# Order of VectorE's work in the ticks that hold both a mix and a last-stage piece

## The chip, the cores and the metric

The kernel runs on one core of a Trainium2 chip. The metric is the device time of one execution in microseconds (us), as the median of several runs. Views of the trace count time from the first instruction of the span. The engines are TensorE (PE for its matmuls, PEld for its weight loads), VectorE (DVE), ScalarE (ACT), GpSimd (POOL) and SyncE (SP, which only issues DMAs).

## The reference, cut to what matters

```python
X = np.fft.rfft(x, axis=1)                 # x: 4 x 3008 x 256, along the sequence
Yr = Xr @ w_r - Xi @ w_i + b_r             # the "mix"
Yi = Xr @ w_i + Xi @ w_r + b_i
Yr = np.sign(Yr) * np.maximum(np.abs(Yr) - 0.01, 0.0)   # soft threshold, Yi likewise
y = np.fft.irfft(Yr + 1j * Yi, n=3008, axis=1)
h = y.reshape(12032, 256) @ w_in           # 256 -> 2048
out = (h / (1 + np.exp(-h))) @ w_out       # 2048 -> 256
```

The soft threshold is computed as y minus y clipped to plus and minus 0.01.

## The kernel before, in words

The Fourier transform and its inverse are each done in two stages of small matmuls, with scratch in DRAM between the stages. Behind them comes the MLP, over 24 blocks of 512 of the 12032 rows (the last has 256), each in 16 slices of the hidden dimension. A block and a slice make one **tick**, and the main loop at the end of the kernel runs over some 380 ticks. Up to block 10 a tick sends to TensorE, in this order: the first product of this tick (`mlp1`, six matmuls of L599), what the schedule `fill` holds for the tick, and the second product of the tick two before (`mlp2`, eight matmuls of L757 and L761). A tick so filled is 4.5 to 6.5 us of TensorE's time.

All engines take their instructions in the order in which the program issues them; `manual_schedule` leaves that order alone. What `fill` holds is set by a planner ahead of the loop, one thing a tick:

- `stack_product` (a "piece" of the forward transform): two matmuls (L293) into two PSUM banks, each followed by a ScalarE copy (L294) and a VectorE addition (L295). Before it stands `stack_split`, a ScalarE copy (L283) and a VectorE subtraction (L284).
- `u3_step` half 0, a "step": `s2_3` (eight matmuls, L390, into one bank, read by ScalarE at L398 and L399 and by VectorE at L400 and L402), `split_z` (L447, L448), and `i1` (six matmuls, L462, into the next bank, copied by ScalarE at L466). The first three steps of a batch have no `i1`, the last three have no `s2_3`.
- `u3_step` half 1, a "mix" (`mix3`): 18 matmuls (L415). The first six go to one bank, which ScalarE copies to the tile q (L421); POOL adds the biases there (L422, L423). The other twelve go to a second bank, `pv`. What is left is the closure `shrink`, which is put on the list `deferred`: four VectorE additions of q and `pv` (L434, 64x256 each), a clip (L437) and a subtraction (L438). After the four additions the second bank is free.

`bank()` gives the banks of these three in turn from two tags, d0 and d1, of one bank each. So a piece or a step that stands in the tick after a mix takes for its first bank the one that q was copied from, and for its second bank the mix's `pv`.

The last stage of the inverse transform builds the next block's input for the MLP, in three calls a block: `i2` for each half of the 256 columns, and `i2_ends` for the remainder of the block before and the block's last, partial piece of the transform. `i2` is four to eight matmuls (L524, L531) into a bank of the tag h, a ScalarE copy (L559) and a VectorE subtraction (L563). `i2_ends` first does L559 and L563 on the remainder in SBUF (`rest`), then the matmuls, L559 and L563 on the new bank (`i2e`), and last a ScalarE copy of what is over into a new `rest` (L579). `mlp1` takes its banks from the same tag h, which has two.

The planner puts some of these calls into a tick that has a mix or a step already. They then have the time t + 0.5 in `fill`, and stand behind the second product on TensorE. There are 20 such ticks, in blocks 2, 3 and 5 to 9 (they prepare blocks 3, 4 and 6 to 10). In 19 of them the other occupant is a mix; in one it is a step. Of the 19, 13 hold an `i2` and six an `i2_ends`. Of the tick that follows,

- eight hold a `stack_product` (six of them after an `i2`, two after an `i2_ends`),
- eight hold a step with both `s2_3` and `i1` (six after an `i2`, two after an `i2_ends`),
- three hold a step with only one of the two, which takes only the first bank (one after an `i2`, two after an `i2_ends`).

In the loop before, the closures on `deferred` are called at the top of the next tick, ahead of `split_g` (ScalarE's L615 and VectorE's L616 of the tick before):

```python
while deferred:
    deferred.pop(0)()
if t and ticks[t - 1][0] not in FAST:
    split_g(*ticks[t - 1])
```

Of the kernel before, what the change touches and what calls it, by code (L numbers as in the profile page):

```python
# [149 lines left out]
def spectral_mlp_kernel(ctx: ExitStack, tc: tile.TileContext, x, w_r, w_i, b_r, b_i, w_in, w_out, c1, c2, c3, c4, c3f, c5, out):  # L150
# [43 lines left out]
    def flush(n):  # L194
        for dst, src in stores[:n]:
            nc.sync.dma_start(out=dst, in_=src)
        del stores[:n]
# [208 lines left out]
    deferred = []  # L406
# [185 lines left out]
    def mlp1(i, f):  # L592
        n = BLOCKS[i][1]
        h, l = xt[i]
        p = ps.tile([128, 512], F32, tag="h", bufs=2, name="h")
        m = 0
        for e in range(2):
            for w, v in ((win[0], h), (win[1], h), (win[0], l)):
                nc.tensor.matmul(  # L599
                    out=p[:, :n], lhsT=w[:, e, f * 128:(f + 1) * 128], rhs=v[:, e, :n],  # L600
                    start=(m == 0), stop=(m == 5),
                )
                m += 1
        g = sb.tile([128, 512], F32, tag="g", bufs=3, name="g")
        for q in halves(i, f):
            nc.scalar.activation(out=g[:, q], in_=p[:, q], func=ACTF.Silu)  # L606
        gf[i, f] = g

    def split_g(i, f):
        n = BLOCKS[i][1]  # L610
        g = gf[i, f]
        gh = sb.tile([128, 512], F32R, tag="gh", bufs=3, name="gh")
        gl = sb.tile([128, 512], F32R, tag="gl", bufs=3, name="gl")
        for q in halves(i, f):
            nc.scalar.copy(gh[:, q], g[:, q])  # L615
            nc.vector.tensor_sub(gl[:, q], g[:, q], gh[:, q])  # L616
        gf[i, f] = (gh, gl)
        units.extend((i, f, t) for t in range(n // 128))
# [71 lines left out]
    def fast_one(i, q):  # L690

        px = fast_bank()
        fast_product(px[:, 0:HB], i, q, 0, 0, True)
        fast_product(px[:, HB:BLK], i, q, 1, 1, False)
        fast.append([i, q, px])

    def fast_more():

        i, q, px = fast[-1]
        py = fast_bank()  # L700
        fast_product(py[:, 0:HB], i, q, (0, 0), (0, 0), True)
        fast_product(py[:, HB:BLK], i, q, 2, 2, False)
        u = tl.tile([128, HB], F32, tag="u", bufs=2, name="u")
        g = tl.tile([128, 4, HB], F32, tag="gp", bufs=3, name="gp")
        nc.scalar.copy(u, py[:, 0:HB])
        nc.vector.tensor_tensor(out=u, in0=px[:, HB:BLK], in1=u, op=ALU.add)
        nc.vector.tensor_tensor(out=g[:, 3, :], in0=px[:, 0:HB], in1=u, op=ALU.add)
        nc.vector.tensor_tensor(out=g[:, 3, :], in0=py[:, HB:BLK], in1=g[:, 3, :], op=ALU.add)
        fast[-1] += [u, py, g]

    def fast_two():

        i, q, px, u, py, g = fast.pop(0)
        fast_product(px[:, 0:HB], i, q, 3, (1, 1), False)
        nc.vector.tensor_tensor(out=g[:, 1, :], in0=px[:, 0:HB], in1=u, op=ALU.add)  # L715
        fast_product(py[:, 0:HB], i, q, (1, 0), (1, 0), False)
        fast_product(py[:, HB:BLK], i, q, (1, 1), 3, False)
        nc.scalar.activation(out=g[:, 1, :], in_=g[:, 1, :], func=ACTF.Silu)  # L718
        nc.scalar.activation(out=g[:, 0, :], in_=py[:, 0:HB], func=ACTF.Silu)  # L719
        nc.vector.tensor_tensor(out=g[:, 2, :], in0=py[:, HB:BLK], in1=u, op=ALU.add)  # L720

        def parts(r):
            h, l = [tl.tile([128, 2, HB], F32R, tag=f"g{k}", bufs=4, name=f"g{k}") for k in "hl"]
            v = g[:, 2 * r:2 * r + 2, :]
            if r:
                nc.scalar.activation(out=v, in_=v, func=ACTF.Silu)  # L726
            nc.scalar.copy(h, v)  # L727
            nc.vector.tensor_sub(l, v, h)  # L728
            gf[i, 2 * q + r] = tuple(a.rearrange("p a c -> p (a c)") for a in (h, l))
            units.extend((i, 2 * q + r, t) for t in range(BLK // 128))  # L730

        parts(0)
        later.append(lambda: parts(1))
# [114 lines left out]
    with tc.manual_schedule():  # L848
# [154 lines left out]
        fill = {}  # L1003
# [14 lines left out]
        def last_stage(i, first):  # L1018

            at(first - 2, i2_load, i)  # L1020
            put(first, i2, i, 0)
            put(first + 2, i2, i, 1)
            at(first + 2, i2_load, i, True)
            return put(first + 4, i2_ends, i)
# [29 lines left out]
        done, t, since = 37, 24, 0  # L1054
# [38 lines left out]
        for i in range(FAST[0], len(BLOCKS)):  # L1093
            if i in FAST:
                first = max(16 * i - 13, last + 1)
                t = last_stage(i, first)
# [19 lines left out]
        def fills(t):  # L1116
            for fn, args in fill.pop(t, []):
                fn(*args)
            if t == int(t):
                flush(1 if t < 12 else 4)  # L1120

        def run(n):
            for v in units[:n]:
                mlp2(*v)
            del units[:n]

        def rest_of_pair():
            while later:
                later.pop(0)()

        first_fast, last_fast = 16 * FAST[0], 16 * (FAST[-1] + 1)
        for t in range(len(ticks) + 1):
            i, f = ticks[t] if t < len(ticks) else (LAST, None)
# [4 lines that stand above are left out]
            if i in FAST:  # L1138
                q = t - first_fast
                if f % 2 == 0:  # L1140
                    state["fast"] = True
                    fast_one(i, f // 2)
                    run(2)
                    if q:
                        fast_two()
                        run(2 if q > 2 else 0)
                else:
                    fast_more()
                    if f != 3:
                        rest_of_pair()  # L1150
                    run(2 if q < 4 else 4)
                    rest_of_pair()
                fills(t)
                continue
            if t == last_fast:
                run(2)
                fast_two()
                run(3)
                rest_of_pair()
            if f is not None:  # L1160
                mlp1(i, f)
            fills(t)
            if last_fast <= t < last_fast + 3:
                run(3 if t == last_fast else 4)
            else:
                run(sum(v[:2] != ticks[t - 1] for v in units))
            fills(t + 0.5)
        run(len(units))
        for k, (dst, src) in enumerate(stores):
            eng = nc.scalar if k % 2 else nc.sync  # L1170
# [28 lines left out]
```

## Time and profile before

| | |
|---|---|
| median of 3 runs | 1353.79 us |
| lowest and highest | 1353.29, 1356.28 us |
| the profiled execution | 1358.12 us |
| its span, first to last instruction | 1355.0 us |
| mean granted clock of TensorE | 0.997 |
| TensorE matmuls busy | 1327.7 us, 98% of the span |
| VectorE busy | 892.1 us, 66% |
| ScalarE busy | 803.7 us, 59% |

The profiled execution holds the span and 3.1 us around it. A row of a timeline has the start, the duration, the engine, the line, the operation, the tiles (out<-in), the shape and the count; in brackets stand the engine's idle time before the row and what ended it.

### The profile page before, as it was taken

The page shows a single profiled execution, that of the slowest core. Times are in us where ns is not written, and L with a number is a line of the kernel's source. Part 1 is how long each engine was busy: PE and PEld are TensorE (multiplying, and loading weights), DVE is VectorE, ACT ScalarE, POOL GpSimd, SP SyncE. Part 2 cuts the span into 40 slices and gives each one's busy share as a digit, 9 for nine tenths or more (in the row PEclk, how much of TensorE's full clock was granted, in tenths as well). Part 3 has the DMA queues.
Part 4 walks back from the last instruction along what each step waited for, and adds up shares of the span by engine and source line. Part 5 has one row for each costly group of instructions (what it writes and reads, how often), then busy time and mean ns, then how long its engine had stood idle before and what let it go on. Part 6 is the DMA issues. An engine that isn't in the chain of part 4 may idle for free.

```text
span 1355.0 us, 22638 instructions
## 1 busy us (share of the span) xinstructions
PE 1327.7 (98%) x8365; PEld 1180.3 (87%) x8365; DVE 892.1 (66%) x1704; ACT 803.7 (59%) x1690; POOL 209.7 (15%) x312
## 2 busy tenths in 40 slices
PE   8989999999999999999999999999999999999998
PEld 3967888888888888888988889999999999999998
DVE  3867746776666777756656756666666666666663
ACT  5546555655676766654554656666666665666555
POOL 2001002221112222111210102111111111111100
PEclk9999999999999999999999999999999999999999
DMA  8875514352436554332331110011001100110000
GB/s 267 264 217 176 140 54 110 97 138 65 114 101 170 126 129 124 93 115 81 106 93 38 46 31 4 28 31 31 7 17 46 31 19 14 31 31 13 5 23 24
DMA packets 76123, 109.98 MB, mean 81 GB/s; under 512 B 8854, under 2 KB 54798, under 8 KB 76014
## 3 DMA queue, kind: packets, MB, share of 16 engines
q1 hardware_dynamic: 61895, 79.17, 20.3%
q0 software_dynamic: 10544, 25.68, 7.8%
q10 hardware_dynamic: 3575, 3.70, 0.9%
q8 instruction: 66, 1.08, 0.3%
q14 instruction: 43, 0.35, 0.1%
HBM read 71.03 MB, written 37.49 MB: 80 GB/s over the span
## 4 chain that ended last, share of the span: by engine, by line
PE 92%; DMA 4%; DVE 2%; ACT 1%; issue 1%; SPq 0%; ACTq 0%; DVEq 0%
PE acc L757 25%; PE h L599 18%; PE h L680 17%; PE acc L761 13%; PE mix L415 6%; PE s L390 2%; PE i L462 2%; PE i2e L531 2%; PE i L531 1%; PE mix L354 1%; DMA scr<-i1o 1%; PE s L293 1%; DVE y L434 1%; DMA scr<-s1o 1%; PE acc L752 1%; DMA t3f<-in_c3f_dram 1%
## 5 line engine op out<-in xcount | busy, mean ns | idle before, releaser
L757 PE MATMUL acc<-wout,gh 128*128 128x512 f32 x1472 | 539.7, 397 | 0.3 <-ACT gh L615 0.3
L761 PE MATMUL acc<-wout,gl 128*128 128x256 f32 x1472 | 414.0, 281 | 0.2 <-DVE gl L616 0.2
L757 PEld LDWEIGHTS acc<-wout,gh 128*128 128x128 f32 x1472 | 278.2, 189 | 48.5 <-ACT gh L615 0.5
L599 PE MATMUL h<-xt,win 128*128 128x512 f32 (+1 forms) x1152 | 290.8, 388 | 0.0
L761 PEld LDWEIGHTS acc<-wout,gl 128*128 128x128 f32 x1472 | 277.5, 189 | 4.6 <-DVE gl L616 0.5
L599 PEld LDWEIGHTS h<-xt,win 128*128 128x128 f32 x1152 | 198.6, 188 | 39.5 <-DVE xt L563 0.4
L606 ACT ACTIVATE g<-h 128x512 f32<-128x512 f32 (+2 forms) x193 | 111.4, 578 | 170.5 <-PE h L599 168.9
L616 DVE TENSOR_TENSOR gl<-g,gh 128x512 fp32r<-128x512 f32 (+2 forms) x193 | 128.2, 666 | 57.0 <-ACT gh L615 55.4
L728 DVE TENSOR_TENSOR gl<-gp,gh 128x512 fp32r<-128x512 f32 x192 | 137.1, 714 | 29.4 <-ACT gh L727 29.4
L718 ACT ACTIVATE gp<-gp 128x256 f32<-128x256 f32 x96 | 40.1, 417 | 163.4 <-DVE gp L715 163.4
L727 ACT CAST gh<-gp 128x512 fp32r<-128x512 f32 x192 | 119.0, 620 | 6.1
L615 ACT CAST gh<-g 128x512 fp32r<-128x512 f32 (+2 forms) x193 | 116.2, 602 | 1.4
L680 PE MATMUL h<-xt,win 128*128 128x256 f32 x576 | 100.7, 284 | 0.5 <-DVE gp L715 0.5
L422 POOL TENSOR_TENSOR q<-q,bias 128x256 f32<-128x256 f32 x36 | 30.9, 859 | 383.1 <-ACT q L421 373.8
L720 DVE TENSOR_TENSOR gp<-h,u 128x256 f32<-128x256 f32 x96 | 40.8, 425 | 72.6 <-ACT gp L719 72.6
L680 PEld LDWEIGHTS h<-xt,win 128*128 128x128 f32 x576 | 81.9, 189 | 5.0 <-DVE gp L715 1.0
L680 PE MATMUL h<-th,sw_h 128*128 128x256 f32 x288 | 84.3, 293 | 0.0
L680 PE MATMUL h<-th,sw_l 128*128 128x256 f32 x288 | 81.6, 283 | 0.0
L680 PE MATMUL h<-tl,sw_h 128*128 128x256 f32 x288 | 81.0, 281 | 0.0
L434 DVE TENSOR_TENSOR y<-q,mix 64x256 f32<-64x256 f32 x144 | 60.3, 419 | 22.1 <-PE mix L415 16.8
L715 DVE TENSOR_TENSOR gp<-h,u 128x256 f32<-128x256 f32 x96 | 40.7, 424 | 50.4 <-PE h L680 50.1
L726 ACT ACTIVATE gp<-gp 128x512 f32<-128x512 f32 x96 | 61.3, 638 | 0.0
(175 smaller groups left out, 2375.3 us busy)
## 6 DMA issues: line engine op xcount, KB each, us to landing
a<-scr SPq DMA_DIRECT2D x48, 256.0 KB
x_sb<-in_x_dram POOLq DMA_DIRECT2D x64, 188.0 KB, 3.8
gin<-scr SPq DMA_DIRECT2D x48, 192.0 KB
t<-in_c_dram POOLq DMA_DIRECT2D x36, 256.0 KB, 3.6
scr<-i1o SPq DMA_DIRECT2D x36, 256.0 KB
t<-in_c_dram SPq DMA_DIRECT2D x48, 128.0 KB
scr<-s1o SPq DMA_DIRECT2D x32, 192.0 KB
scr<-s1o SPq DMA_DIRECT2D x13, 384.0 KB
```

Of the source, the lines that this page charges most:

```text
L415: nc.tensor.matmul(out=out, lhsT=x_[:, e, c, :], rhs=m[:, e, :], start=(n == 0), stop=(n == 5))
L434: nc.vector.tensor_tensor(out=y[64 * i:64 * i + 64, r, :], in0=q[rows, i, :], in1=pv[rows, i, :], op=op,)
L599: nc.tensor.matmul(out=p[:, :n], lhsT=w[:, e, f * 128:(f + 1) * 128], rhs=v[:, e, :n], start=(m == 0), stop=(m == 5),)
L606: nc.scalar.activation(out=g[:, q], in_=p[:, q], func=ACTF.Silu)
L615: nc.scalar.copy(gh[:, q], g[:, q])
L616: nc.vector.tensor_sub(gl[:, q], g[:, q], gh[:, q])
L680: nc.tensor.matmul(out=p, lhsT=w[j], rhs=m[k], start=(begins and n == 0), stop=(n == 2), skip_group_check=True,)
L726: nc.scalar.activation(out=v, in_=v, func=ACTF.Silu)
L727: nc.scalar.copy(h, v)
L728: nc.vector.tensor_sub(l, v, h)
L757: nc.tensor.matmul(out=a, lhsT=gh[:, q], rhs=wout[:, f].rearrange("p a c -> p (a c)"), start=begins, stop=False,)
L761: nc.tensor.matmul(out=a[:, D:2 * D], lhsT=gl[:, q], rhs=wout[:, f, 0, :], start=False, stop=ends,)
```

## The change

In a tick that has something at t + 0.5, the closures on `deferred` are called ahead of it, and no longer at the top of the next tick. So in the 19 shared ticks with a mix, the six VectorE instructions of `shrink` stand ahead of the L563 of the piece (in `i2_ends`, ahead of both). In all other ticks the program is the same. No instruction is added or taken away, and the order on every other engine and on every DMA queue stays.

```diff
                 run(sum(v[:2] != ticks[t - 1] for v in units))
-            fills(t + 0.5)
+            if t + 0.5 in fill:
+                while deferred:
+                    deferred.pop(0)()
+                fills(t + 0.5)
         run(len(units))
```

## Rows read from the trace of the kernel before

**Rows 1.** The page, busy time, share of the span and instructions of each engine.

```profile
PE 1327.7 (98%) x8365; PEld 1180.3 (87%) x8365; DVE 892.1 (66%) x1704; ACT 803.7 (59%) x1690; POOL 209.7 (15%) x312
```

**Rows 2.** The waits of PE: who waited for whom, us in total, times, longest.

```profile
PE s L293 <- DVE y L434: 8.8, 8, 1.3
PE i L462 <- PE s L390: 4.5, 8, 0.8
```

**Rows 3.** Groups by form, DVE, 200 to 735 us: busy us, mean ns | idle before.

```profile
L434 DVE TENSOR_TENSOR y<-q,mix 64x256 f32<-64x256 f32 x144 | 60.3, 419 | 22.1 <-PE mix L415 16.8 <-POOL q L422 3.4
...
L438 DVE TENSOR_TENSOR y<-y,q 128x512 f32<-128x512 f32 x36 | 24.9, 693 | 1.2
...
L437 DVE TENSOR_SCALAR q<-y 128x512 f32<-128x512 f32 x36 | 15.4, 428 | 1.2
```

**Rows 4.** Timeline of a mix that shares its tick with nothing, 200 to 215.

```profile
201.60 0.74 POOL L423 TENSOR_TENSOR q<-q,bias 128x256 f32<-128x256 f32 x1
...
201.84 1.72 DVE L434 TENSOR_TENSOR y<-q,mix 64x256 f32<-64x256 f32 x4 [2.43 <-PE mix L415]
```

**Rows 5.** Timelines of POOL, DVE and PE: a shared tick (i2), then stack_product.

```profile
298.53 1.21 POOL L422 TENSOR_TENSOR q<-q,bias 128x256 f32<-128x256 f32 x1 [11.79 <-ACT q L421]
299.81 0.73 POOL L423 TENSOR_TENSOR q<-q,bias 128x256 f32<-128x256 f32 x1
...
301.39 0.40 DVE L563 TENSOR_TENSOR xt<-i,xt 128x235 fp32r<-128x235 f32 x1 [2.25 <-ACT xt L559]
...
302.19 0.40 PE L293 MATMUL s<-sx,c_sb 111*128 111x512 f32 x1
303.67 0.47 PE L293 MATMUL s<-sx,c_sb 111*128 111x512 f32 x1 [1.08 <-DVE y L434]
303.98 0.40 PE L757 MATMUL acc<-wout,gh 128*128 128x512 f32 x1
```

**Rows 6.** Timeline of PE: a stack_product and a step without a wait.

```profile
519.27 0.63 PE L293 MATMUL s<-sx,c_sb 111*128 111x512 f32 x2
519.74 0.39 PE L757 MATMUL acc<-wout,gh 128*128 128x512 f32 x1
...
251.65 1.05 PE L390 MATMUL s<-t,a 128*128 128x128 f32 x8
252.46 0.36 PE L462 MATMUL i<-zh,t 128*128 128x256 f32 x1
```

**Rows 7.** Timelines of PE and DVE: the step after a shared tick (i2).

```profile
699.96 1.05 PE L390 MATMUL s<-t,a 128*128 128x128 f32 x8
701.82 0.36 PE L462 MATMUL i<-zh,t 128*128 128x256 f32 x1 [0.82 <-PE s L390]
...
700.01 1.72 DVE L434 TENSOR_TENSOR y<-q,mix 64x256 f32<-64x256 f32 x4
```

**Rows 8.** Timelines of POOL, DVE, ACT: i2_ends of block 3, then stack_product.

```profile
243.42 1.21 POOL L422 TENSOR_TENSOR q<-q,bias 128x256 f32<-128x256 f32 x1 [9.27 <-ACT q L421]
...
246.23 0.41 DVE L563 TENSOR_TENSOR xt<-i2e,xt 128x242 fp32r<-128x242 f32 x1 [1.26 <-ACT xt L559]
...
246.67 0.35 ACT L579 COPY rest<-i2e 128x228 f32<-128x228 f32 x1 [0.48 <-DVE xt L563]
...
248.06 0.58 ACT L294 COPY s1o<-s 48x512 f32<-48x512 f32 x1
...
250.21 1.28 DVE L295 TENSOR_TENSOR s1o<-s,s1o 48x512 f32<-48x512 f32 x2
```

**Rows 9.** Timelines of DVE and ACT: i2_ends of block 7, then a step.

```profile
510.53 1.73 DVE L284 TENSOR_TENSOR sx<-x_sb,sx 47x1024 fp32r<-47x1024 f32 x1 [2.29 <-ACT sx L283]
512.29 0.43 DVE L563 TENSOR_TENSOR xt<-rest,xt 128x258 fp32r<-128x258 f32 x1
...
513.86 0.30 ACT L579 COPY rest<-i2e 128x174 f32<-128x174 f32 x1 [0.53 <-DVE xt L563]
...
518.70 0.57 ACT L466 COPY i1o<-i 128x512 f32<-128x512 f32 x1
```

## The prediction

> **What bounds the kernel now.** First the page's busy times. TensorE is busy for 98% of the span and VectorE for 66% [rows 1], so a reordering on VectorE is worth only what it takes out of TensorE's 27 us of idle time (1355.0 less 1327.7). Then the waits of TensorE, and of these the two that fall into the ticks with a mix [rows 2]. The second matmul of a `stack_product` (L293) waited 8 times for VectorE's L434, for 8.8 us in all. The first matmul of `i1` (L462) waited 8 times, 4.5 us in all, and the view puts that down to the step's own L390. Eight and eight are also the numbers of shared ticks that are followed by a piece, and by a step with both of its parts. Last the timelines of one such tick of each sort.
>
> In rows 5 the shared tick's piece ends its VectorE subtraction (L563) at 301.79. Only then do the four additions of the mix begin. They hold the second bank for 1.7 us (4 at 0.42 us [rows 3]), to about 303.5, and L293, which wants that bank, starts at 303.67. VectorE had stood idle for 2.25 us before that L563, since the piece's matmuls are the last of TensorE's tick and ScalarE copies them first.
>
> In rows 7 the view names L390, but L390 was through at 701.01, while the four additions ran from 700.01 to 701.73 and L462 started at 701.82. The bank that `i1` takes is the mix's second one. I read these eight waits too as waits for L434.
>
> **What the change does, part by part.**
>
> *The additions, moved ahead.* In a tick that the mix has to itself nothing stands ahead of the additions, and they start as soon as the mix's last matmul is through: VectorE was idle until then, and the additions ran beside POOL's second bias addition (L423, to 202.34) without waiting for it [rows 4]. In the shared tick of rows 5 POOL's first addition (L422) was stretched to 1.21 us and ended at 299.74, and L423 ended at 300.54. The first two additions need L422, the other two L423. So they would run from 299.78 to 300.63 and from there to 301.5. Clip and subtraction (0.43 and 0.69 us [rows 3]) bring `shrink` to its end at 302.7.
>
> *The stall that goes.* L293 wants the bank at 302.42 (302.19 and one matmul's pitch of 0.23), and the additions are through at 301.5. The wait is covered with 0.9 us to spare. What one such wait costs is more than the idle time that the view shows, because a matmul's modelled end runs into it. From the first L293 to the L757 behind the pair it was 303.98 − 302.19 = 1.79 us here, and 519.74 − 519.27 = 0.47 us without a wait [rows 5, 6]: 1.32 us lost for 1.08 shown. For `i1`, from the first L390 to the first L462, it was 701.82 − 699.96 = 1.86 us against 252.46 − 251.65 = 0.81: 1.05 lost for 0.82 shown [rows 6, 7]. Each of the 16 waits is worth 0.24 us more than its row: 8.8 + 4.5 + 16 × 0.24 = 17.1 us.
>
> *The piece's L563, moved back.* In the 13 ticks with an `i2` it can start when `shrink` ends: 302.7 for 301.39 in rows 5, 1.3 us later. What is late next is the bank of the tag h that it reads, which `mlp1` of the tick after next wants. That is one `mlp2` (1.4 us) behind L293's pair, at 302.66 + 1.4 = 304.07; L563 ends at 303.1. The next tick's L616 comes no later than before, since the work ahead of it is the same. These 13 cost nothing; the cover is 1 us, and the loss would begin past it.
>
> *ScalarE behind L579.* In the six ticks with an `i2_ends` ScalarE's copy of the remainder (L579) starts only when VectorE's last L563 has ended: 246.64 and 246.67 in rows 8, and again in rows 9. Now both L563 stand behind `shrink`, and behind L579 ScalarE's queue holds the gh of this tick, the Silu of the next and the copies of the next piece or step. This part works against the change.
>
> For block 3 [rows 8]: L422 ends at 244.63, the additions run to 246.4, `shrink` to 247.6. The L563 on the remainder I take at 0.43 us, the time of the one in rows 9, to 248.0; the last one (0.41) ends at 248.3, so L579 starts 1.65 us later than at 246.67. Then the first L294 starts at 249.7 for 248.06 and ends at 250.3. Its L295 (half of 1.28) ends at 251.0. TensorE, without its stall 1.34 us ahead (idle 1.10 and 0.24), wants the first bank for the next step's L390 at 251.65 − 1.34 = 250.3 [rows 6], and gets it 0.1 us behind L295, at 251.1. Of 1.34 us it keeps 0.5: 0.8 is given back. The lower end is nothing given back (the bound of 17.1), the upper all 1.34.
>
> For block 7 [rows 9] VectorE is busy with L284 to 512.26, and the additions can begin only then: `shrink` ends at 515.2, the two L563 at 516.05, L579 starts at 516.05 for 513.86, 2.2 us late. The step's copies shift with it: L398, L399, VectorE's L400 and L402 behind them, L401, L447, and L466 at 519.5 for 518.70. The next tick's L293 wants its banks at 519.27 − 0.75 = 518.5 (idle 0.50 and 0.24 gained). The first comes free behind L402 at 519.4, the second behind L466 at 520.2, where the row of before has the second L293 at 519.50. So this tick gains 0.75 and gives back 1.45, a loss of 0.7.
>
> Block 4's `i2_ends`, also followed by a `stack_product`, has the pattern of block 3, but the step behind has no `s2_3`, and its `i1` comes to the bank at the same place; I estimate 0.3, between nothing and block 3's 0.8. After block 9's the next thing is a mix, which wants no bank before ScalarE has caught up, and blocks 8 and 10 had no wait to win and follow with a step of six matmuls: nothing given back there.
>
> *A shared port.* POOL's L422 took 1.21 us where L423 took 0.73 [rows 5], the same shape. The Trainium skill, "SBUF — State Buffer", "Who interferes with whom", says that a VectorE operation with two SBUF inputs and a GpSimd operation that reads SBUF exclude each other, and that one with a single SBUF input doesn't. Rows 4 agree for L434, which reads q and a PSUM bank. The L563 on the remainder reads two SBUF tiles, so by that rule it may last longer beside POOL; had it needed another 0.5 us in blocks 3 and 4, the sum would be 1 us smaller. It now comes after POOL is done, so I keep the 0.43.
>
> **Sum.** 17.1 − 0.8 − 1.45 − 0.3 = 14.6 us. No instruction is added and no DMA is issued elsewhere in a queue. The profiled execution took 1358.1 us, 1355.0 of them the span, and would take 1343.5. It lies 4.3 above the median of the runs, and I know of nothing in these ticks that makes the difference, so I carry the 14.6 over to the median: 1353.79 − 14.6 = 1339.2 us. Behind the last mix the chain is TensorE's to the end, so what is won is kept.
>
> **The rivals.**
>
> *Nothing given back.* L579 waits for less than the last L563, or ScalarE's lateness meets no bank: 17.1 us, 1336.7. Against it: L579 started 0.03 us behind that L563 in rows 8 and 9. Chance 0.08, within the forecast's own range.
>
> *ScalarE gives back more.* If all six `i2_ends` ticks end as block 7's, at −0.7 each, they bring −4.2 in place of +2.1 (0.5, 1.2, −0.7 and 1.07 of blocks 3, 4, 7, 9). The other 12 waits bring 12.5, so 8.3 us: 1345.5. For it: every L579 waits so. Against it: only block 7's has L284 ahead. Chance 0.13.
>
> *The waits of i1 aren't L434's.* Then the view is right and L390 or something behind it holds L462. The eight `stack_product` ticks remain: 6 × 1.32 + 0.5 + 1.2 less block 7's 0.7 give 8.9 us: 1344.9. Against it: the 0.09 us between the additions' end and L462 [rows 7]. Chance 0.05.
>
> *No change.* The additions still start late, because POOL's bias sums come late, and L293 waits as before: 1353.8. Against it: of the 22 us that VectorE idled before L434 only 3.4 were POOL's [rows 3]. Chance 0.03.
>
> *Slower: the h bank.* If `shrink` itself is late by D in its new place, L563 and with it the bank of the tag h are late too. From D = 0.9 us on `mlp1` waits, and the old wait comes back from the same point; past 2.2 us the tick is slower than before, as TensorE then waits for `shrink` and the piece after it. At D = 3 us, 0.8 us lost in each of 19 ticks give 15 us: 1369. That needs POOL's or VectorE's work ahead of the additions to take 3 us more than in rows 5; the latest that I find, block 7's, is 1.7 us behind its mix, for L284. Chance 0.04.
>
> **How the numbers follow.** The forecast has a chance of 0.67, with its own range of 1336.5 to 1342.5. Both middle rivals end near 1345, so the range is 1336.5 to 1345.0; it takes in the bound of nothing given back and about half of those two, and leaves out some 0.15. A measurement of this kernel can tell about 0.2%, 2.7 us, from no change. Faster by more than that are the forecast and the first three rivals, 0.93; within it 0.03; slower 0.04.
>
> **What would show it.** In the profile after, L293's wait for L434 should be gone from TensorE's waits, and `i1`'s too, and TensorE's idle time should fall by over 10 us. L434 should start about 0.1 us behind the mix or behind POOL in all 36 mixes. L563's idle time should fall. In the `i2_ends` ticks L579 should wait longer for L563, 1.6 to 2.2 us in blocks 3 and 7, and new short waits should appear at L390 or L462 behind block 3's and 4's, at L293 behind block 7's. The forecast is wrong if L462 still waits, or if `mlp1` (L599) waits for an h bank in ticks with an `i2`.

## The result, and the profile after

| | before | after |
|---|---|---|
| median of 5 runs, us | 1353.79 | 1342.07 |
| lowest to highest | 1353.29 to 1356.28 | 1339.30 to 1343.07 |
| span of the profiled execution | 1355.0 | 1340.2 |

The ratio is 0.9906, with a 95% interval of 0.9891 to 0.9920: faster by 11.7 us, where 14.6 were forecast, and inside the forecast's range. The interval stands for 10.8 to 14.8 us, so it just takes in the 14.6. The spans of the two profiled executions differ by 14.8 us. The 3 us between these two figures are taken up with the first experiments.

The page after, busy time of each engine; it answers to [rows 1]:

```profile
span 1340.2 us, 22656 instructions
...
PE 1322.7 (99%) x8365; PEld 1178.6 (88%) x8365; DVE 889.2 (66%) x1704; ACT 804.1 (60%) x1690; POOL 209.9 (16%) x312
```

TensorE's idle time fell from 27.3 to 17.5 us, by 9.8, a little less than the "over 10" that the prediction names as a sign; in the stretch with the mixes (200 to 736 us before, 200 to 722 after) it fell from 13.3 to 1.4. Its busy time fell by another 5.0. Part of the second is the waits' too: the prediction counted 0.24 us of pitch for each of 16 waits, 3.8 us, that the view books as busy.

The waits of TensorE after (those above 0.15 us), to be held against [rows 2]:

```profile
PE i L459 <- DVE wout L846: 3.1, 1, 3.1
PE i L524 <- DMA gin<-scr: 2.6, 1, 2.6
...
PE s L293 <- DVE xl L402: 0.7, 1, 0.7
PE s L293 <- ACT i1o L466: 0.3, 1, 0.3
...
PE s L390 <- DVE s1o L295: 0.2, 1, 0.2
```

No wait for L434 is left, and none of L462 for L390. What the change brought are three short waits in the places that the prediction named: L293 twice (block 7) and L390 (block 3); a fourth, of 0.09 us at block 4's L462, is below the view's bound. (L390 also waits once for a DMA, 0.2 us, as it does for 0.6 us in the second profile of the kernel before.) The two long ones at the top lie ahead of the main loop, in code that the change doesn't touch.

Now the tick of [rows 5], after, in the timelines of POOL, VectorE and TensorE:

```profile
296.37 1.21 POOL L422 TENSOR_TENSOR q<-q,bias 128x256 f32<-128x256 f32 x1 [11.77 <-ACT q L421]
...
297.61 1.72 DVE L434 TENSOR_TENSOR y<-q,mix 64x256 f32<-64x256 f32 x4 [0.63 <-POOL q L422]
299.36 0.43 DVE L437 TENSOR_SCALAR q<-y 128x512 f32<-128x512 f32 x1
299.82 0.69 DVE L438 TENSOR_TENSOR y<-y,q 128x512 f32<-128x512 f32 x1
300.54 0.41 DVE L563 TENSOR_TENSOR xt<-i,xt 128x235 fp32r<-128x235 f32 x1
...
300.02 0.63 PE L293 MATMUL s<-sx,c_sb 111*128 111x512 f32 x2
300.49 0.39 PE L757 MATMUL acc<-wout,gh 128*128 128x512 f32 x1
```

The additions start 0.03 us behind POOL's L422, stretched to 1.21 us as before, and end at 299.33; both L293 now stand in one row, and L757 follows 0.47 us behind the first, as in the undisturbed pair of [rows 6]. L563 starts behind `shrink`, at 300.54, and no matmul waits for it. VectorE's idle time before L563, in the stretch with the mixes, fell from 52.0 us to 0.2. The step of [rows 7] after:

```profile
687.51 1.05 PE L390 MATMUL s<-t,a 128*128 128x128 f32 x8
688.32 0.36 PE L462 MATMUL i<-zh,t 128*128 128x256 f32 x1
...
684.02 1.71 DVE L434 TENSOR_TENSOR y<-q,mix 64x256 f32<-64x256 f32 x4 [1.73 <-PE mix L415]
```

From L390 to L462 it is 0.81 us, the undisturbed distance of [rows 6]. Block 3's `i2_ends`, which answers to [rows 8]:

```profile
242.89 1.72 DVE L434 TENSOR_TENSOR y<-q,mix 64x256 f32<-64x256 f32 x4 [0.63 <-POOL q L422]
...
245.71 0.47 DVE L563 TENSOR_TENSOR xt<-rest,xt 128x312 fp32r<-128x312 f32 x1
246.22 0.41 DVE L563 TENSOR_TENSOR xt<-i2e,xt 128x242 fp32r<-128x242 f32 x1
...
246.66 0.35 ACT L579 COPY rest<-i2e 128x228 f32<-128x228 f32 x1 [1.69 <-DVE xt L563]
...
248.06 1.07 ACT L294 COPY s1o<-s 48x512 f32<-48x512 f32 x2
...
248.67 1.28 DVE L295 TENSOR_TENSOR s1o<-s,s1o 48x512 f32<-48x512 f32 x2 [0.41 <-ACT s1o L294]
...
249.41 1.16 PE L390 MATMUL s<-t,a 128*128 128x128 f32 x8 [0.16 <-DVE s1o L295]
```

ScalarE waits 1.69 us at L579, with gh, Silu and the two L294 behind it, and L390 waits for the L295 that comes out of them. And block 7's, to be held against [rows 9]:

```profile
506.50 0.30 ACT L579 COPY rest<-i2e 128x174 f32<-128x174 f32 x1 [2.74 <-DVE xt L563]
...
509.90 0.58 ACT L466 COPY i1o<-i 128x512 f32<-128x512 f32 x1
...
509.78 0.47 PE L293 MATMUL s<-sx,c_sb 111*128 111x512 f32 x1 [0.65 <-DVE xl L402]
510.53 0.50 PE L293 MATMUL s<-sx,c_sb 111*128 111x512 f32 x1 [0.28 <-ACT i1o L466]
```

To see what each place gave, I took from both traces the start of the first L599 of every tick and subtracted; what changes from one tick to the next is that tick's gain. The eight places at L293 gave 1.31 to 1.50 us each, 10.8 in all, the eight at L462 0.59 to 1.06, 6.3 in all: 17.1. Given back were 0.41 (block 3), 0.38 (block 4) and 1.44 (block 7), 2.2 in all. These places together gained 14.9 us. The whole loop, from its first L599 to the end of the span, gained 14.4: ticks that the change doesn't touch, the first of the loop and the one at 421.6 us with the DMA wait of L390, lost 0.5 on balance.

### The profile page after: what moved, and what is told of

The parts are those of the page before. It is cut to its first block, busy times and chain, and to the rows that moved or that the text cites. A ratio compares the mean times of both kernels' runs of the same rounds, so it can differ in the third digit from the quotient of the medians.

```text
span 1340.2 us, 22656 instructions
## 1 busy us (share of the span) xinstructions
PE 1322.7 (99%) x8365; PEld 1178.6 (88%) x8365; DVE 889.2 (66%) x1704; ACT 804.1 (60%) x1690; POOL 209.9 (16%) x312
## 4 chain that ended last, share of the span: by engine, by line
PE 90%; DMA 4%; ACT 2%; DVE 2%; issue 1%; SPq 0%; POOL 0%; ACTq 0%; DVEq 0%
PE acc L757 24%; PE h L680 18%; PE h L599 17%; PE acc L761 12%; PE mix L415 5%; PE s L390 2%; PE i L462 2%; PE mix L354 2%; PE i L531 1%; PE i2e L531 1%; DMA scr<-i1o 1%; PE s L293 1%; DMA scr<-s1o 1%; DMA a<-scr 1%; PE acc L752 1%
## 5 line engine op out<-in xcount | busy, mean ns | idle before, releaser
L757 PE MATMUL acc<-wout,gh 128*128 128x512 f32 x1472 | 539.6, 397 | 0.1
L757 PEld LDWEIGHTS acc<-wout,gh 128*128 128x128 f32 x1472 | 277.9, 189 | 49.0 <-issue 0.5
L599 PE MATMUL h<-xt,win 128*128 128x512 f32 (+1 forms) x1152 | 290.8, 387 | 0.0
L599 PEld LDWEIGHTS h<-xt,win 128*128 128x128 f32 x1152 | 198.3, 188 | 39.8 <-DVE xt L563 0.4
L434 DVE TENSOR_TENSOR y<-q,mix 64x256 f32<-64x256 f32 x144 | 60.3, 419 | 45.1 <-PE mix L415 36.6
L422 POOL TENSOR_TENSOR q<-q,bias 128x256 f32<-128x256 f32 x36 | 31.1, 862 | 369.9 <-ACT q L421 361.6
```

The lines of the kernel that those rows point to most:

```text
L434: nc.vector.tensor_tensor(out=y[64 * i:64 * i + 64, r, :], in0=q[rows, i, :], in1=pv[rows, i, :], op=op,)
L599: nc.tensor.matmul(out=p[:, :n], lhsT=w[:, e, f * 128:(f + 1) * 128], rhs=v[:, e, :n], start=(m == 0), stop=(m == 5),)
L757: nc.tensor.matmul(out=a, lhsT=gh[:, q], rhs=wout[:, f].rearrange("p a c -> p (a c)"), start=begins, stop=False,)
```

## The experiments

The theory: L293 and L462 wait for the bank that L434 frees; the full change takes all 16 waits, and gives some back where ScalarE is held at L579. The rivals: L462 waits for something else; what is given back comes by VectorE's own lateness; the gain is the 11.7 us of the medians, and the traces flatter it. Each run is compared with the kernel before on the same chip. Beside the runs "ahead of an i2_ends only", "one buffer" and "later still" the kernel before had a median of 1358.11 us (13 runs), beside the other four 1354.59 (17 runs).

### The kernel before, once more

> The kernel before once more, for its spread. The profiled execution of before was 4.3 us above its median, and the two traces differ by 14.8 us where the medians differ by 11.7. Theory: the difference lies in stretches that the change does not touch (the loads ahead of the main loop), so the 16 waits at L293 and L462 are here again at 13.3 us of TensorE idle within 0.5, while the span differs by 1 to 4 us from 1355.0. Rival: the waits themselves vary from run to run, and here they sum to some 10 us, which is the 11.7 of the medians.

Median 1356.33 us (1353.10 to 1360.29, 12 runs), span 1354.2. The waits of TensorE:

```profile
PE s L293 <- DVE y L434: 8.8, 8, 1.3
PE i L462 <- PE s L390: 4.5, 8, 0.8
...
PE s L390 <- DMA a<-scr: 0.6, 1, 0.6
PE mix L415 <- DVE s1o L295: 0.3, 1, 0.3
```

The median is 1.7 us above that of the same kernel in the 17 runs beside it, so differences of that size between medians show little. The 16 waits are the same to 0.1 us. The span came out 0.8 us from the other, short of the 1 us expected, but as the sum of two opposite differences: the main loop's first L599 stood at 103.36 us instead of 105.81, and two waits not there before, of 0.6 us for a DMA and 0.3 behind it, were added in the loop.

### The changed kernel, once more

> The changed kernel once more. Theory: some 1342 us, idle time of TensorE between 200 and 722 us again 1.2 to 1.5 us, 11 to 15 us under the kernel before on the same chip. Rival (the gain is 11.7 and the traces flatter it): idle time of 4 us or more in that stretch.

Median 1341.02 us (1339.19 to 1345.10, 6 runs), ratio 0.9900 (0.9884 to 0.9917), 13.6 us under before. The three new waits are again 0.64, 0.29 and 0.16 us, with one of 0.39 for a DMA: with the one at L462 1.6 us of idle time in the stretch, a little over what was expected, against the 4 us of the rival. By this the traces don't flatter the gain: the waits are gone in both. The stretch from the first L599 to the end of the span is the loop without what lies ahead of it:

| profile | first L599 | span | difference |
|---|---|---|---|
| before | 105.81 | 1355.0 | 1249.2 |
| before, again | 103.36 | 1354.2 | 1250.8 |
| after | 105.44 | 1340.2 | 1234.8 |
| after, again | 107.49 | 1342.0 | 1234.5 |

The loop is 14.4 to 16.3 us shorter; the larger figure holds, for the most part, the two extra waits of the second profile of before. By the interval of the ratio the medians differ by 11.2 to 15.7 us here, so they don't contradict the 14.4. Over all nine profiles of this study its start lies between 102.3 and 107.5 us. That spread of 5 us is more than the 3 us in question. Only the profiled runs have a trace, so how much of it fell on each median isn't shown.

### Ahead of an i2 only

```diff
             if t + 0.5 in fill:
-                while deferred:
+                while deferred and fill[t + 0.5][0][0] is i2:
                     deferred.pop(0)()
```

> The additions go ahead only of an i2, not of an i2_ends. Theory (ScalarE is held behind L579, and the six i2_ends ticks bring 0.9 + 1.1 - 0.7 + 1.0 = 2.3 us net): 12.5 us under before, 2.3 us over the full change; the waits at L390, L462 and L293 that were new are gone, and four of the old waits are back (1.1, 1.3, 0.5, 0.8 us). Rival (the i2_ends ticks bring nothing or a loss): the same as the full change or up to 4 us faster.

Median 1344.09 us (1341.22 to 1345.05), ratio 0.9909 (0.9893 to 0.9926): 10.5 us under before (12.5 were expected) and 3.1 over the full change on the same chip. By tick starts it is 2.3 us behind the full change, as expected: 1.33, 1.48, 0.74 and 1.03 lost, 0.42, 0.38 and 1.44 won back. The waits:

```profile
PE s L293 <- DVE y L434: 2.4, 2, 1.3
...
PE i L462 <- PE s L390: 1.3, 2, 0.8
```

So the `i2_ends` ticks together still bring something, and block 7's alone is a loss.

### Ahead of an i2_ends only

The same edit, with `i2_ends` in place of `i2`.

> The additions go ahead only of an i2_ends, not of an i2. Theory: the four waits behind an i2_ends go (4.65 us with their pitch), and 0.4, 0.4 and 1.4 us are given back at L390, L462 and L293: 2.4 us under before; the twelve waits behind an i2 stay, at 8.7 us of idle time. Rival (ScalarE's lateness adds up over blocks): no gain or a loss.

Median 1355.01 us (1352.69 to 1355.80), ratio 0.9976 (0.9964 to 0.9988), 3.1 us under before by the medians, where 2.4 were expected. By tick starts it is 1.8: 1.34, 1.48, 0.74 and 1.05 won, 1.00, 0.38 and 1.42 given back. Block 3 gave back 1.00, not the 0.41 of the full change. The rows of that tick:

```profile
242.43 1.21 POOL L422 TENSOR_TENSOR q<-q,bias 128x256 f32<-128x256 f32 x1 [9.28 <-ACT q L421]
...
243.68 1.72 DVE L434 TENSOR_TENSOR y<-q,mix 64x256 f32<-64x256 f32 x4 [0.63 <-POOL q L422]
...
250.20 1.16 PE L390 MATMUL s<-t,a 128*128 128x128 f32 x8 [0.69 <-DVE s1o L295]
```

The mix's last matmul ends at 242.42 here and at 242.21 in the full change, but POOL's L422 starts 0.77 us later, at 242.43 instead of 241.66, and the additions with it. The cause lies in the step one mix earlier. There L401, ScalarE's copy of what VectorE's L400 has made, waits for it; the rows are of the kernel before, of this run and of the full change:

```profile
239.69 0.41 ACT L401 CAST xh<-xs 128x256 fp32r<-128x256 f32 x1 [1.66 <-DVE xs L400]
...
238.70 0.41 ACT L401 CAST xh<-xs 128x256 fp32r<-128x256 f32 x1 [1.67 <-DVE xs L400]
...
237.93 0.41 ACT L401 CAST xh<-xs 128x256 fp32r<-128x256 f32 x1 [0.49 <-DVE xs L400]
```

Where block 3's second `i2` still stands ahead of the additions, VectorE comes to L400 late and ScalarE waits 1.17 us longer than in the full change, while TensorE loses 0.62 there. The difference, 0.55 us, is how much later against the mix ScalarE's q, and with it POOL, is in this tick.

### The remainder's copy ahead of the subtraction, one buffer

```diff
+            nc.scalar.copy(h[q], p[:, :, 0:m])
-            split_x(i, p[:, :, 0:m], (slice(None), slice(None), slice(o, o + m)))
...
             nc.scalar.copy(rest[i + 1], p[:, :, m:z])
+            nc.vector.tensor_sub(l[q], p[:, :, 0:m], h[q])
```

(The fast blocks keep the old order.)

> The full change, and in i2_ends the remainder's copy (L579) stands ahead of the last VectorE subtraction, but both subtractions stay behind the additions. The remainder has one buffer, so the copy still waits for the first of the two. Theory (ScalarE's wait at the copy sets what is given back): the copy comes 0.45 to 0.5 us earlier, the waits of L390 (0.16) and L462 (0.09) go, and at block 7's L293 0.5 of 0.93 us goes: 1.3 us under the full change, 0.9 over the version that also frees the first subtraction. Rival (VectorE's lateness): all waits as in the full change, same time.

Median 1340.84 us (1339.36 to 1342.08), ratio 0.9877 (0.9862 to 0.9892). That is 17.3 us under before, more than the next version's 15.9 on another chip, so the medians can't show the 0.9 us that were expected between the two. Against the full change the tick starts are 0.41, 0.36 and 0.49 us ahead at blocks 3, 4 and 7: 1.26 us for the 1.3 expected. The waits at L390 and at block 4's L462 are gone, and at block 7 the first L293 waits 0.15 instead of 0.65 us, the second 0.29 as before.

### Both freed

The edit above, and in an `i2_ends` tick the first L559 and L563 (on the old remainder) are called ahead of `deferred`:

```diff
             if t + 0.5 in fill:
+                if fill[t + 0.5][0][0] is i2_ends:
+                    i2_rest(*fill[t + 0.5][0][1])
                 while deferred:
```

> The full change, and in i2_ends the remainder's copy (L579) stands ahead of the last VectorE subtraction in ScalarE's queue and the subtraction on the old remainder ahead of the mix's additions. Theory (what was given back came by ScalarE waiting at the remainder's copy): the new waits at L390 (0.16), L462 (0.10) and L293 (0.65 and 0.28) go, 2.2 us under the full change. Rival (VectorE's own lateness behind the additions gives it back): the waits stay, and the time is that of the full change.

Median 1338.69 us (1336.72 to 1339.38, 4 runs), ratio 0.9876 (0.9860 to 0.9891): 15.9 us under before, 2.3 under the full change on the same chip. The tick starts are 0.41, 0.36 and 1.43 us ahead of the full change's, 2.2 as expected, and all four new waits are gone. Block 7's tick, ScalarE (the copy is L587 here, the L559 ahead of it L585):

```profile
499.25 0.41 ACT L585 CAST xt<-i2e 128x296 fp32r<-128x296 f32 x1 [2.12 <-PE i2e L531]
499.55 0.31 ACT L587 COPY rest<-i2e 128x174 f32<-128x174 f32 x1
499.75 0.63 ACT L625 CAST gh<-g 128x512 fp32r<-128x512 f32 x1
```

The copy no longer waits, and the last L563 is as late as ever, behind `shrink`. So it was ScalarE's wait, not VectorE's lateness. Of the three changed versions timed on this chip this one has the lowest median, and by tick starts it is the fastest too.

### The additions later still

```diff
-            while deferred:
-                deferred.pop(0)()
             if t and ticks[t - 1][0] not in FAST:
                 split_g(*ticks[t - 1])
+            while deferred:
+                deferred.pop(0)()
```

> The kernel before, with the additions put later still: at the top of the next tick they come behind L616 of split_g in place of ahead of it, in every tick. Theory (the 16 waits are for the second bank, which L434 frees): in the shared ticks L616 waits for an L615 that stands behind the piece on ScalarE, so each wait of L293 and of L462 grows, by some 0.75 us behind an i2 and 1.5 us behind an i2_ends: 12 x 0.75 + 4 x 1.5 = 15 us, 1369 us. Mixes that have the tick to themselves lose nothing, since there L615 is done before the mix ends. Rival (the waits of L462 are L390's own): L293's eight grow and L462's stay, 7.5 us, 1362 us. Rival (L434 is not what either waits for): no change.

Median 1384.89 us (1383.68 to 1390.27, 4 runs), ratio 1.0212 (1.0185 to 1.0239): 26.8 us slower than before by the medians, not 15. Its waits of TensorE:

```profile
PE s L293 <- DVE y L434: 17.1, 9, 2.8
PE i L462 <- issue: 11.9, 8, 2.2
...
PE mix L415 <- ACT i1o L466: 1.9, 2, 1.1
```

The waits grew as the theory has it, L293's by 8.3 us (a new ninth wait of 0.28 among them) and L462's by 7.4, together 15.7 for 15 expected; L462's growth is against the rival that gives those to L390. The view names no one for L462 now, but here too it starts 0.10 us behind the end of the additions:

```profile
223.05 1.72 DVE L434 TENSOR_TENSOR y<-q,mix 64x256 f32<-64x256 f32 x4
...
224.87 0.36 PE L462 MATMUL i<-zh,t 128*128 128x256 f32 x1 [1.19 <-issue]
```

Most of the rest is TensorE's clock. Stretches of this run; the columns are the stretch, its length, the busy times of PE, PEld, DVE, ACT and POOL (with their instructions), the granted clock, the DMA share and GB/s.

```profile
248.10:254.90 6.80, 6.19 (x18) 5.15 (x19) 3.45 (x7) 1.38 (x3) 0.00 (x0) 0.50 0.33 89
309.50:312.90 3.40, 3.40 (x12) 2.72 (x11) 1.60 (x3) 0.26 (x1) 0.00 (x0) 0.50 0.25 58
...
664.50:667.90 3.40, 3.40 (x14) 3.01 (x13) 2.97 (x7) 1.93 (x4) 0.00 (x0) 0.50 0.00 0
sum 23.80, PE 23.19 PEld 19.36 DVE 16.73 ACT 7.83 POOL 0.51; mean PE 3.87 PEld 3.23 DVE 2.79 ACT 1.30 POOL 0.09
```

In these and three more, six in all, the granted clock was at half, 1.2 GHz, and TensorE busy for 23.2 of 23.8 us. What that costs can be read from the six L599 of a tick, in the second stretch and just behind it at 2.4 GHz (rows of the chain that ended last):

```profile
310.33 2.56 PE h L599 x6
...
315.98 1.40 PE h L599 x6
```

At 1.40 for 2.56 some 10.5 of the 23.2 us are lost, an estimate from these two rows; the tick starts give 10.5 as well, once the growth of the waits is taken off. With 15.7 and the new waits of L415, 1.9, that makes 28.1. The loop, from the first L599 (102.90) to the end (1381.9), took 1279.0 us, 29.8 more than the 1249.2 of before; the last 1.7 were not followed up. The expectation of 15 us had the waits right and left the clock out.

## Why the prediction was right

**The waits and their owner.** L462's wait was read as L434's from 0.09 us between two rows, against the name in the view. After the change, which moves nothing but `shrink` against L563, all eight are gone, and with the additions moved the other way they grew. That is shown.

**What a wait costs.** 17.1 us were forecast, from the view's waits and the 0.24 us that two pairs of rows showed beside them; the 16 places gave 17.1.

**The piece's L563.** No L599 matmul waits in the stretch with the mixes of the profile after, as said; the 13 `i2` ticks cost nothing. The slower rival had no part in it.

**ScalarE behind L579.** The mechanism was right, and the two runs that free the copy show it. The sum of the three terms was 2.55 us, 2.2 were measured: block 7 1.45 against 1.44, block 4 0.3 against 0.38, block 3 0.8 against 0.41. Block 4's 0.3 had no working of its own, so that it came near is partly luck. Block 3's term was mis-sized: L579 was to wait 1.65 us longer and waited 1.21 longer (1.69 for 0.48). (By its own terms, 248.0 and 0.41, the last L563 would end at 248.4 and not 248.3, which makes the term a little larger still.) It took POOL's L422 at its distance from the mix in the trace of before. There the additions one mix earlier, late behind their own `i2`, had held ScalarE and POOL back against TensorE, and the change moves those too. With them left late, the tick gave back 1.00.

**The shared port.** The term for the L563 on the remainder was kept at 0.43 us; it took 0.47. The rule of the Trainium skill cited there is borne out most plainly by block 10's remainder of 6 columns, which ran beside POOL's L422 (718.23 to 718.96) before and behind POOL's additions after:

```profile
718.26 0.72 DVE L563 TENSOR_TENSOR xt<-rest,xt 128x6 fp32r<-128x6 f32 x1 [0.23 <-ACT xt L559]
```

in the kernel before, and in the kernel after

```profile
707.48 0.16 DVE L563 TENSOR_TENSOR xt<-rest,xt 128x6 fp32r<-128x6 f32 x1
```

**The sum.** 14.6 us were forecast for the ticks that the change touches, and these gained 14.9; the medians moved by 11.7 in the first comparison and 13.6 in the second. The forecast carried the ticks' gain over to a median of few runs as if the rest of the time stood still, while the start of the loop alone varies by 5 us between profiles. The measured 1342.07 lies 2.9 us above the 1339.2 and only 0.4 inside the upper end of the forecast's own range, 1342.5. That it fell inside is partly luck: the prediction names no term for this spread.

## What to carry to other kernels

Where an engine waits for a bank, ask which reader frees it and what stands ahead of that reader in its queue, whatever name the view gives. A ready instruction that stands behind one that must wait for the end of the tick can be put ahead; in 13 of the 19 ticks here that cost nothing. Then follow what was put back: in the other six a copy on another engine stood behind it, and that engine's whole queue with it; giving that copy its place ahead brought the last 2.2 us. Working out such a chain from the trace of before, remember that an earlier delay which the change also removes has shifted the engines against each other there.

## What the runs showed of the hardware that wasn't expected

The late version has ten waits of TensorE of 1.88 us and more. With six of them its granted clock came down to 1.2 GHz, for 3.4 us in five places and 6.8 us in one; with four of them, one of 2.80 us among these, and with the 16 waits (1.26 us and less) of the kernel before, it stayed at 2.4. What tells the six from the four wasn't tried. At the second place the clock fell at 309.5, 1.4 us after the wait had ended at 308.15 and while TensorE was working. So moving the additions back by one VectorE instruction cost nearly twice what the waits themselves grew by, 29.8 us of loop for 15.7 of waits.

The VectorE subtraction of 6 columns that took 0.72 us beside a POOL addition took 0.16 us without one.
